# Retention and token/channel mixer on one core: two u turns by crossbar, a last chain in halves, another order

## The chip, the cores and the metric

The kernel runs on one core of a Trainium2 chip. The metric is the device time of one execution in microseconds; of several executions the median is given. A separate execution is profiled: its page and its trace are what the sections below read. Engines are TensorE (PE, with its weight loads as PEld), VectorE (DVE), ScalarE (ACT), GpSimd (POOL) and SyncE (SP); POOL, SP and ACT also issue DMAs.

## What is computed

For each of 4 batches and 8 heads (sequence 768, head size 64) a decaying state is carried along the sequence, and its output goes through a mixer over tokens and one over channels:

```python
gamma = 1.0 - 2.0 ** (-5.0 - np.arange(H, dtype=np.float32))
for t in range(S):
    state = gamma * state + k[:, :, t] (outer) v[:, :, t]
    y[:, :, t] = scale * q[:, :, t] @ state
...
xt = x.transpose(0, 2, 1)                  # x: heads side by side, 512 wide
h = np.maximum(xt @ w_tok1, 0.0) @ w_tok2  # 768 -> 256 -> 768
u = x + h.transpose(0, 2, 1)
h2 = np.maximum(u @ w_ch1, 0.0) @ w_ch2    # 512 -> 1536 -> 512
return u + h2
```

(The two lines in the loop are abridged.) Inputs and output are float32, products run on float16.

## The kernel before

The sequence is cut into six chunks of 128, the heads into four pairs of 128 rows. For each batch b and pair p, `front(b, p)` does the retention and the token mixer; for each batch, `back(b)` does the channel mixer.

**front.** q, k and v come by POOL's DMAs, which convert to float16 (`load`); only k of pair (0,0) comes through SP as float32. `decayed` scales k, and q where it will be turned by crossbar, by powers of the head's gamma (L530 on ScalarE, L532 on VectorE). `turn` brings k and q into columns: by six or twelve TensorE transposes and a copy out of PSUM (modes "t" and "w"), or by a crossbar DMA on SP (mode "x", L544). The table `TURNS` gives a mode for k, q and u of each pair: batches 0 and 1 have `twt`, batches 2 and 3 `xxx`. Then: state contributions per chunk (L586, half the array's columns at a time), a first copy and four decaying sums on VectorE (L596, L598), crossing states (L616, L618), scores (L637, half the rows), the mask (L648), y from scores and from states (L668, L694), copies out (L710), the token mixer (L725, relu L734 or L736, L745), and u (L710), which is turned too: by six transposes (L790) with a copy (L796), or by crossbar (L780).

**back.** The first channel product ("widen") is done plainly for batch 0 (L824, relu L840); batches 1 to 3 save one product in eight by sums and differences of blocks (`widen7`): differences of u on VectorE (L863), products (L893), kept parts copied by ScalarE (L904), added (L913) and clipped in place (L917) by VectorE. The first product of a batch waits for u of all its four pairs. The second product ("narrow") is done in the same way for block pairs (`narrow7`: sums L1007, chains of six matmuls of 256 columns L1043 and L1053, kept parts L1033, additions into X L1060, and a store of 128 rows, 256 KB, L1086). For the last batch, blocks 4 and 5 go plainly through `narrow` (L969, L978, store L984), the last of them in column pieces of 256, 128 and 128.

**Order.** Every piece of work is an `Op` with one or more ways (an engine, a cost in ns, the code that issues it). Two long strings give the order of all of them (`ORDERED`, an index of two digits each) and the way of each (`WAYS`). `arrange` walks through the order with a model of engines, PSUM banks, buffers and DMA rings to place banks and buffers, and each engine gets its instructions in that order, in its own queue; an engine waits at each instruction until what it needs is there. Until 21 us of planned time, fill matmuls on a zero tile (L1168) are put where the plan has gaps on TensorE.

**Constants.** `away` (POOL iota, L402) is a table of column minus row; from it come the logarithms `lgs` of the decays (eight memsets L408, a product L410 on VectorE), and from these the factors `gk` for k (L414) and `gy` for q (L415) on ScalarE, the identity (L418) and the mask (L444). `late`, q's decay along the chunk, is four exponentials on ScalarE (L435).

Of the kernel before, what the change touches and what calls it, by code (L numbers as in the profile page):

```python
# [9 lines left out]
FP = mybir.dt.float32  # L10
# [28 lines left out]
class Rings:  # L39
# [67 lines left out]
INTO, OUT_OF = 92, 111  # L107
FREE = dict(PE=300, ACT=2500, DVE=900, POOL=900, SP=750)


def arrange(ops, BANKS, seq, ways):
# [82 lines left out]
    while left:  # L194
        moved = False
        wake = INF
        for e in ENGINES:
# [61 lines left out]
    "0b05040a07000d0103020e060c1e0h1f1i0f1j1g1h0j08090g1t1k1x1s1l0i1O1m1w1P1n1v0l1Q1o1u1S1R1p1y1T0o1z1q1U1r1V221W"  # L259
    "230n2o1A1X242p1Y0m1C1Z2q26202s272r1B2t0k1D2Y252C2D2Z0q2F2u212H302v2G28312a2w292E0r2b2c1E2x2y0t2I2z1F2d342A35"  # L260
    "0p2B1J362e37380s2K1G2f2M2J392L1H2g3a0w2N321I1K2j332h2O0v2i1L3c2P4K0A2k3e3d3b2Q3f2m3h0u2R2T2l3g3i3k1M2U3m3j3l"
    "0z2V1N5j3n3C4L3y3o2S0y3z2W2n3p3A47483q2X0x3t5k3r493u3E3B0E3s3w3vac3xaf3F3GaM3HaN3DadaPaO0Dagaear4aaxah3IaQ0C"
    "3Jas3Mat4baR3Pb73Qb8b13Nau0B3Oavb24cawaD3KaJ0Gayb3aGb9aKazao0F3L4laLaH4oap4n0L4daq3R3TaI4eaA1a3VaBaS4H4GaT4f"
    "ai4maUaj0H4gaE4pak4I4hal4i4J1bbjamaFaVbkan1d3SaC0JbaaWbm3Ubbbo3Wb4aXaYbnb5bc1caZ4jbg0Nb0bd16bh3Xbi0K17b6be3Y"
    "bqbl18bf0I3Z4UbI40bObr19410R424k4Y4M5fbvbP4V4r4t4Nbw4q6p4sbx4X0M4u4Obz4v4Pby43154Wbs5Obp45bA4Q44bBbJ5gbt4w46"
    "4RbKbE4xbL4SbTbCbF4T4Z50bU4y5P0T5152bD4z5Q5l5U4A5m4B0O535V5h5W4CbX5n5X540Pc44DbM5o5ibY555Y5pbNc56mc85q5Z56bR"
    "bu6qc65r575R5Sc95t5sbS5T5a585vcd6n5ubV6r5wce605y5x5AchbQ5C6oc7bW5z5Bci5b0Q6s6Uc06t5D594E5c0U6ucmc17s6v6V5E6w"
    "12cn4F6xcfbZ5F0S617t62cg5G6y640W5J5H665dcj655K145I635e5Mck68670X5N69ca6bcl5L6a0Vcb6A6ccqcu6X6C6d6Y6DcNcc6Z6e"
    "cLcrcvcwcM6B6f6z6WczcscQcxcA6icRct707u6gcCcOcTcD6EcBcUcScycocEcJ806GcV6I6jd0716hcKcGd1cXcH81d26FcY6kdR116H72"
    "d3d4cW736Jd9cZ74d7dS13d5dT6KdWd8d6dU7y7vda757zdX6L7AdbcFcPdZ767Bdcdhe0dY7w6Mde7C0Z7xdie1e683djcI7De3dfe76N6l"  # L270
    "e4dk78dV77dAdd7cdoc2dB6Q7bcp6OdC7982dpdFe5dq6RdDdldG7adrdIdEdsdm7e7gdJdHdt6S86dn84dydK7d7f87dzdP850Y886PdMdL"
    "89ey7hdu8adQe26TdNdv7ieWdg8yeu7j7EdwbGez8bc3eUeX7kev8B7Gew8C7l7K7FeDeQ8zeFdOdxeE7I8A7oeV7meGeHex7peJeS8c7reR"
    "7qeAeI7J7nf1eB8D96eK7M7O7HeMeLbHeZeNf27L7Nf0eC8e107Pe8f37Q8i99f58ff48h7R9a8g8dee9be97Secf697ef9E7TeY8jea8k7U"
    "7Wf7ed8m7V8Eeg9c7XeTej9H7Z9d8F7Y8l9eeh8G9f8Hf898ekeieb8nen8I8of9el9g8J9h8peoemfc8Mep8q8Keq8O8L8r8Qfg8P8s8uer"
    "fx8t8Nfh9kfdfyfi8v9nflfjfCfmfz9mfD8Sfofe8wfO9lfpfF9F8R9ofvfGfA8U9G8Tfn9ifffE8VfqfMfwg58xfH8Wfs9IfN9Kft9jfJ9J"
    "8X9Lfkg6fKfQ9MfP8Ygaetfug7fRgbfT9N9qgdfU9O9p9PeO9r8Zg8gegc9Q90fW9t9s92fX9ufVgfgk91g3fY93ghfIg4g0fBgi949vglg1"
    "gD9w9SgEg2fSgmgg9R9UgIgn9xg9fZgFgJ9Tgr9y9VgLgsgtfrgGgMgKgu9z9W9XgN9ZgvgSgogwgTgBa19AgxgOgCgPfLgp9YgyhChIhEa0"
    "hGgza2gjhNhDhHgQa3gqgHhLhOa4hg9BhRhM9DhFa5hPhJa6hifbgYhSgRhrgAhQhha8hUhTa9hkhsabgUhvgVgZa7h095hK9Ch3hlh1hjfa"
    "hmh4gWePhphnh2h5hqhogXh7h6hth8hVh9huhwhchxhyhahYi2hZiAhbi3ijaai4hdi7ikhei0ilesi8i5iohAi9hzipiahWimhfiqhXi1ir"
    "ibiHisicihiTitiiieivifiRiwiCiBj8iSiFiYiDiGiWiUhBiyi6iIiXidjaixiziJiZjfiKj0kEiPiMj1iQj6iNj3jpj2j9j4koj7jdjbjq"  # L280
    "jrinjejwjujsjgjvkMkNkpjhjciEjxiVjtjniLjyjKiujojEigjik6jFjzjkjjkqjAjlkFkOkwk2kPkQkGjBk3k7kriOjCkRksjmkbk4jDkt"
    "j5kcjGkdjHjLkHkIkfkejIjPkSkujMjJkvjRjNkTk5khjQkgjSjTkijVkjjUkJkxkmjWjYjOkKk8jXkLkyjZkzk0k9kAk1kBkkkakCklkDkn"
)
WAYS = (
    "000000000000000000000000000000000000000000000000000000000000000000000000000010000000000000000000000000000010"
    "010100000000000000000000000001010000000100000000000000000000000000000000000100000000000010000000000010000000"
    "000101010000000000000000000000000000000010100000000000000000000000000000001000000000000000000000000000010100"
    "000000000000001000000000000000000001010110000000000000000000000000000000010000000000000000000000000000000000"
    "000000000000000000000000000000010010000000000000000000000000000000000000000000000000000000000000000000000000"
    "000000000000000010000000000000000000000000000000001000000000001000000010000000000000000000000000000000000000"  # L290
    "000000000000000000000000000000000000000000000000000000000000000000000000000011000000000000000000001100000000"
    "000000000000110000000000000000000010000000000000000000000000000000000000000000000000000000000000000000000000"
    "000000000000000000000000000000001100000000000000000000000000000000000000000010000000000000000000000000000000"
    "000000000000000001000000000000000000000000000000000000000000000000000000000000000000000000100000100000000000"
    "000000000010000000000010001000001100000000000000000000000000000000000001000000000000000000100000000000000000"
    "000010000000001000000100000000000000000000000000000010000000000000000000000100000000000000000000000100000000"
# [4 lines left out]
def kernel(  # L301
# [43 lines left out]
    TURNS = "twt twt twt twt twt twt twt twt xxx xxx xxx xxx xxx xxx xxx xxx".split()  # L345
# [39 lines left out]
    lgs = const_p.tile([P, H], FP, name="lgs")  # L385
    lnsc = const_p.tile([P, 1], FP, name="lnsc")
# [31 lines left out]
    ident_op = prep("DVE", 330, lambda: nc.vector.tensor_scalar(ident16, away, 0.0, None, ALU.is_equal), [away_op],  # L418
                    (-20, 0, -1, 1))
# [781 lines left out]
```

## Time and profile before

| | |
|---|---|
| median of 3 runs | 187.42 us (186.85 to 187.65) |
| profiled execution | 186.83 us |
| its span, first to last instruction | 185.0 us |
| granted TensorE clock | 0.996 |
| instructions | 5291 |
| moved by DMA | 24.91 MB in 92248 packets |

The page gives busy time by engine, the span in 40 slices, the DMA queues, and the chain of work that ended last, followed back from the last instruction. A matmul's duration holds its way through the array, so that neighbours overlap; what one costs in a row of matmuls is the distance from start to start. The chain of waits gives each piece from its release on. Every time in a timeline counts from the span's start.

### The profile page before, as it was taken

The numbers are of one execution on the slowest core, as the hardware profiler recorded it, in microseconds if no ns is written. First come the engines' busy times: TensorE is split into PE (matmuls) and PEld (weight loads), VectorE is DVE, ScalarE is ACT, GpSimd is POOL, SyncE is SP. The second block draws the span as 40 slices with busy tenths as digits, with TensorE's granted clock in tenths as the row PEclk, the third lists the DMA queues.
The fourth block names the chain that finished last, engine by engine and source line by source line (L and its number), as shares of the span: only waits on it lengthen the run. The fifth ranks groups of instructions, "written<-read, shape, count | busy, mean of one in ns | idle before, by whom it ended". The sixth has DMA issues, their size and how long they took to land.

```text
span 185.0 us, 5291 instructions
## 1 busy us (share of the span) xinstructions
PE 177.1 (96%) x2089; PEld 134.6 (73%) x2089; DVE 170.2 (92%) x466; ACT 133.4 (72%) x304; POOL 53.6 (29%) x63
## 2 busy tenths in 40 slices
PE   7788899999999999999999999999999999999991
PEld 3456788656689988866668898667679986567881
DVE  4599799859999999999999999999999999999992
ACT  5689698469789899999999697898864416552120
POOL 8994786355424609704220020000000000000000
PEclk9999999999999999999999999999999999999998
DMA  6999999999999999999999995027002444500035
GB/s 117 143 160 176 199 170 198 194 189 206 167 157 154 121 156 123 156 148 185 146 233 161 190 138 100 4 43 198 3 0 40 123 143 174 225 0 0 4 142 198
DMA packets 92248, 24.91 MB, mean 135 GB/s; under 512 B 81984, under 2 KB 89280, under 8 KB 92224
## 3 DMA queue, kind: packets, MB, share of 16 engines
q0 software_dynamic: 67728, 13.18, 89.8%
q1 hardware_dynamic: 23056, 9.11, 25.4%
q10 hardware_dynamic: 1440, 2.29, 3.3%
q8 instruction: 16, 0.26, 0.6%
q14 instruction: 8, 0.07, 0.1%
HBM read 26.74 MB, written 6.29 MB: 179 GB/s over the span
## 4 chain that ended last, share of the span: by engine, by line
PE 69%; DVE 16%; POOL 6%; DMA 5%; issue 2%; ACT 1%; POOLq 0%
PE bank L893 18%; PE bank L1043 11%; PE bank L824 9%; PE bank L1053 9%; DMA wt<-in_moe_w_tok_dram 5%; PE bank L745 5%; PE bank L725 4%; DVE X L1060 4%; DVE am L648 4%; DVE hs L1007 3%; PE bank L969 3%; DVE h L913 2%; POOL v L492 2%; PE bank L668 2%; PE bank L637 2%; PE bank L694 2%
## 5 line engine op out<-in xcount | busy, mean ns | idle before, releaser
L648 DVE TENSOR_TENSOR am<-bank,mask 128x384 f16<-128x384 f32 x64 | 32.9, 547 | 2.9 <-PE bank L637 2.8
L913 DVE TENSOR_TENSOR h<-bank,us 128x384 f16<-128x384 f32 x54 | 28.8, 551 | 0.6 <-PE bank L893 0.2
L904 ACT COPY us<-bank 128x384 f32<-128x384 f32 x50 | 23.3, 489 | 8.3 <-PE bank L893 6.4
L492 POOL DMA_DIRECT2D v<-in_v_dram x16 | 16.5, 1034 | 40.4 <-PE bank L694 25.7
L893 PE MATMUL bank<-hs,late 128*128 128x384 f16 x108 | 22.6, 326 | 0.0
L1033 ACT COPY us<-bank 128x256 f32<-128x256 f32 x30 | 10.7, 373 | 14.5 <-PE bank L1043 9.5
L1043 PEld LDWEIGHTS <-hs 128*128 128x128 f16 x198 | 18.5, 98 | 2.4
L893 PEld LDWEIGHTS <-late 128*128 128x128 f16 x144 | 13.2, 98 | 8.2 <-issue 0.4
L1060 DVE TENSOR_TENSOR X<-X,bank 128x256 f32<-128x256 f32 x44 | 17.7, 412 | 0.8 <-PE bank L1053 0.4
L1043 PE MATMUL bank<-wsum,hs 128*128 128x256 f16 x132 | 17.5, 273 | 0.0
L598 DVE SCALAR_TENSOR_TENSOR U<-U,gp,bank 128x64 f32<-128x64 f32 x64 | 16.8, 274 | 0.7
L710 ACT CAST u<-bank 128x384 f16<-128x384 f32 x31 | 14.6, 487 | 3.9 <-PE bank L745 3.3
L824 PE MATMUL bank<-uT,wc 128*128 128x384 f16 x96 | 16.9, 326 | 0.0
L492 POOL DMA_DIRECT2D k<-in_k_dram x15 | 15.4, 1033 | 4.9 <-DVE am L648 1.4
L710 ACT CAST x<-bank 128x384 f16<-128x384 f32 x30 | 14.1, 483 | 3.6 <-PE bank L694 3.4
L893 PE MATMUL bank<-uT,wc 128*128 128x384 f16 x72 | 16.4, 326 | 0.1
L616 ACT ACTIVATE cross<-U,gp 64x320 f16<-64x320 f32 x29 | 16.2, 559 | 0.4
L745 PE MATMUL bank<-h,wt 128*128 128x128 f16 x192 | 15.7, 219 | 0.3 <-DMA wt<-in_moe_w_tok_dram 0.3
L530 ACT ACTIVATE k<-k,gk 128x384 f16<-128x384 f16 x25 | 14.9, 617 | 1.4 <-DMA k<-in_k_dram 1.1
L840 ACT ACTIVATE h<-bank 128x384 f16<-128x384 f32 x24 | 10.6, 492 | 5.0 <-PE bank L824 4.8
L710 ACT COPY X<-bank 128x384 f32<-128x384 f32 x29 | 14.0, 492 | 0.0
L745 PEld LDWEIGHTS <-wt 128*128 128x128 f16 x192 | 12.3, 98 | 2.2 <-DMA wt<-in_moe_w_tok_dram 0.5
(91 smaller groups left out, 382.8 us busy)
## 6 DMA issues: line engine op xcount, KB each, us to landing
out_dram<-X SPq DMA_DIRECT2D x15, 256.0 KB, 3.1
q<-in_q_dram POOLq DMA_DIRECT2D x16, 192.0 KB, 8.4
v<-in_v_dram POOLq DMA_DIRECT2D x16, 192.0 KB, 7.3
k<-in_k_dram POOLq DMA_DIRECT2D x15, 192.0 KB, 7.9
wc<-in_moe_w_ch_dram POOLq DMA_DIRECT2D x5, 512.0 KB, 13.9
out_dram<-X ACTq DMA_DIRECT2D x8, 256.0 KB, 2.5
wc<-in_moe_w_ch_dram POOLq DMA_DIRECT2D x2, 256.0 KB, 10.6
us<-in_k_dram SPq DMA_DIRECT2D x1, 384.0 KB, 3.4
```

Source lines behind the costliest of these rows:

```text
L492: (nc.sync if hard else nc.gpsimd).dma_start(out=tile_of(s, [P, 2, NC, D], FP if hard else F16), in_=src.rearrange("h (c p) d -> p (h c) d ...
L598: nc.vector.scalar_tensor_tensor(out=u[:, c], in0=u[:, c - 1], scalar=gp[:, p:p + 1], in1=st, op0=ALU.mult, op1=ALU.add)
L648: nc.vector.tensor_tensor(am, SC[g].tile[:, :m * P].rearrange("p (i t) -> p i t", t=P), mask.to_broadcast([P, m, P]), ALU.mult)
L710: (nc.scalar.copy if e == "ACT" else nc.vector.tensor_copy)(tile(), t)
L745: nc.tensor.matmul(Y[j].tile[:, 2 * i * D:2 * (i + 1) * D], wt2[:, jt, t], H1.tile[:, jt], start=False, stop=(jt == NJ - 1), skip_group_ch ...
L824: nc.tensor.matmul(acc[:, :SH], wc1[:, ct, ft * P:(ft + 1) * P], UT.tile[:, ct, sh * SH:(sh + 1) * SH], start=(ct == 0), stop=(ct == NP - 1))
L893: nc.tensor.matmul(acc[:, :SH], left(ct), r[:, ct], start=first and ct == 0, stop=ct == C2 - 1, skip_group_check=True)
L904: (nc.scalar.copy if e == "ACT" else nc.vector.tensor_copy)(ks[:, j], R1.tile[:, :SH])
L913: nc.vector.tensor_tensor(h(m, sh), R.tile[:, :SH], KS.tile[:, j], ALU.add)
L1043: nc.tensor.matmul(acc_[:, lo], l[:, j], r[:, j], start=first and j == 0, stop=j == K2 - 1, skip_group_check=True)
L1053: nc.tensor.matmul(acc_[:, lo], l[:, j], r[:, j], start=first and j == 0, stop=j == K2 - 1, skip_group_check=True)
L1060: (nc.vector if e == "DVE" else nc.gpsimd).tensor_tensor(dst(), dst(), b_(), ALU.add)
```

## The change

- **u by crossbar.** `TURNS` has `twx` for pairs 0 and 1 of batch 1: their u is turned by a crossbar DMA on SP.
- **The last chain in two halves.** In `narrow7` for blocks 2 and 3 of the last batch, the last chain (columns 256 to 511 of block 2) is split into two of 128 columns, each with its own addition and its own store of 64 KB. The first 256 columns of block 2 are stored by themselves (128 KB), block 3 as a whole (256 KB).
- **k decays from ScalarE.** `gk` is computed by one activation from the logarithms (`lnG`) with `away` as its scale; `lgs`, the product on VectorE, is left for `gy` only, and `late` waits for the memsets only.
- **More choice.** The first state copy (L596) and the in-place relu of `widen7` (L917) may also go to ScalarE.
- **Costs and order.** Costs of the planner are changed (among them the price of a change of tile shape on TensorE, and the landing of POOL's loads until 26 us); `ORDERED` and `WAYS` are new throughout. By position, TensorE has 446 groups instead of 447. POOL issues k and q of pair (0,1) and v of pair (0,0) ahead of `away`, q of pair (0,3) ahead of the first token weight, and v of pair (0,3) behind the second. Five stores of batches 1 and 2 stand among the last work of batch 3.

```diff
-            return 1470 if t < 4500 else 2100 if t < 17000 else 1700
+            return 1470 if t < 4500 else 2100 if t < 26000 else 1700
...
-INTO, OUT_OF = 92, 111
-FREE = dict(PE=300, ACT=2500, DVE=900, POOL=900, SP=750)
+CHANGE = {"": 92, "row": 110, "col": 100, "turn": 110}
+FREE = dict(PE=300, ACT=2100, DVE=900, POOL=900, SP=750)
...
-                    s_ = max(t, free[e] + (INTO if o.tiled else 0) + (OUT_OF if tiled == "high" else 0))
+                    s_ = max(t, free[e] + CHANGE[tiled])
...
-    TURNS = "twt twt twt twt twt twt twt twt xxx xxx xxx xxx xxx xxx xxx xxx".split()
+    TURNS = "twt twt twt twt twx twx twt twt xxx xxx xxx xxx xxx xxx xxx xxx".split()
...
-            nc.vector.memset(lgs[:, h:h + 1], math.log(1.0 - 2.0 ** (-5.0 - h)))
+            nc.vector.memset(lnG[:, h:h + 1], math.log(1.0 - 2.0 ** (-5.0 - h)))
         nc.vector.memset(lnsc, math.log(scale))
-        nc.vector.tensor_scalar(lgs, lgs, away[:, MID:MID + 1], -1.0, ALU.mult, ALU.mult)
-    lgs_op = prep("DVE", 450, emit, [away_op])
-
-    def emit():
-        nc.scalar.activation(gk, lgs, AF.Exp, scale=-1.0)
-        nc.scalar.activation(gy, lgs, AF.Exp, bias=lnsc, scale=1.0)
-    g_op = prep("ACT", 380, emit, [lgs_op])
+    logs_op = prep("DVE", 220, emit)
+    lgs_op = prep("DVE", 400, lambda: nc.vector.tensor_scalar(lgs, lnG, away[:, MID:MID + 1], -1.0, ALU.mult, ALU.mult),
+                  [away_op, logs_op])
+    g_op = prep("ACT", 190, lambda: nc.scalar.activation(gk, lnG, AF.Exp, scale=away[:, MID:MID + 1]), [away_op, logs_op])
+    gy_op = prep("ACT", 190, lambda: nc.scalar.activation(gy, lgs, AF.Exp, bias=lnsc, scale=1.0), [lgs_op])
...
-    gq_op = prep("ACT", 2450, emit, [since_op, lnh_op, lgs_op], (-20, 0, -1, 1), [LATE], [SINCE])
+    gq_op = prep("ACT", 2450, emit, [since_op, lnh_op, logs_op], (-20, 0, -1, 1), [LATE], [SINCE])
...
-                    nc.vector.tensor_copy(u[:, 0], st)
+                    (nc.scalar.copy if e == "ACT" else nc.vector.tensor_copy)(u[:, 0], st)
...
-                    def emit():
-                        nc.vector.tensor_scalar(h(m, sh), h(m, sh), 0.0, None, ALU.max)
-                    rel[i + m * M2, sh] = op(one("DVE", (180, 260), emit), [ad], [], [H2s[sh]])
+                    def emit(e):
+                        if e == "ACT":
+                            nc.scalar.activation(h(m, sh), h(m, sh), AF.Relu)
+                        else:
+                            nc.vector.tensor_scalar(h(m, sh), h(m, sh), 0.0, None, ALU.max)
+                    rel[i + m * M2, sh] = op(either(emit, DVE=(167, 250), ACT=act(SH, 0, 1)), [ad], [], [H2s[sh]])
...
-            p3 = chain(lambda: HS.tile[:, 3], w(1, hi), [sm[3], k4] + cw, False, True)
-            o12 = add(part(x0, hi), acc(0, lo), [p3] + xd, [X, banks[0]], FROM_BANK)
...
+            if b == B - 1 and i1 == 3:
+                store(i1, slice(0, C), [y2])
+                store(i0, lo, [y11])
+                got = k4
+                for g in range(2):
+                    cols = slice(g * P, (g + 1) * P)
+
+                    def emit(cols=cols, left=lambda: HS.tile[:, 3], right=w(1, hi)):
+                        l, r = left(), right()
+                        for j in range(K2):
+                            nc.tensor.matmul(banks[0].tile[:, cols], l[:, j], r[:, j, cols], start=False, stop=j == K2 - 1,
+                                             skip_group_check=True)
+                    got = op(one("PE", (336, 500), emit), [sm[3], got] + cw, [], [ha, hb, HS, banks[0]])
+                    last = slice(N2 + g * P, N2 + (g + 1) * P)
+                    o12 = add(part(x0, last), lambda cols=cols: banks[0].tile[:, cols], [got] + xd, [X, banks[0]],
+                              dict(DVE=(200, 284)))
+                    store(i0, last, [o12])
+            else:
+                p3 = chain(lambda: HS.tile[:, 3], w(1, hi), [sm[3], k4] + cw, False, True)
+                o12 = add(part(x0, hi), acc(0, lo), [p3] + xd, [X, banks[0]], FROM_BANK)
+                store(i1, slice(0, C), [y2])
+                store(i0, slice(0, C), [y11, o12])
```

The rest of the diff is the two strings and planner costs that change by a few ns.

More of the change, by code (lines that the diff above doesn't have):

```diff
@@ L264 @@
[L264 to L273, printed above, removed]
@@ L599, in emit @@
                                                    op0=ALU.mult, op1=ALU.add)
-            prev = op(one("DVE", (195, 280) if c else (140, 220), emit), [pp, gp_op, prev], [US] if c == 0 else [],
+            prev = op(either(emit, DVE=(190, 276)) if c else either(emit, DVE=(132, 216), ACT=act(D)), [pp, gp_op, prev], [US] if c == 0 else [],
                       ([] if c == 0 else [US]) + [ST])
@@ L796, in emit @@
                 (nc.scalar.copy if e == "ACT" else nc.vector.tensor_copy)(UT.tile[:, p], T.tile[:, :S])
-            e = op(either(emit, ACT=act(S), DVE=dve(S, 0.54)), [t, None if opens else first_of[b, "uT"]],
+            e = op(either(emit, ACT=act(S), DVE=(467, 550)), [t, None if opens else first_of[b, "uT"]],
                    [UT] if opens else [], [T] if opens else [T, UT])
@@ L1044, in emit @@
                                          stop=j == K2 - 1, skip_group_check=True)
-                return op(one("PE", (655, 815), emit), deps, [banks[0]] if first else [],
+                return op(one("PE", (655, 818), emit), deps, [banks[0]] if first else [],
                           [ha, hb, HS] if first else [ha, hb, HS, banks[0]])
@@ L1054, in emit @@
                                          stop=j == K2 - 1, skip_group_check=True)
-                return op(one("PE", (655, 815), emit), deps, [banks[g]] if first else [],
+                return op(one("PE", (655, 818), emit), deps, [banks[g]] if first else [],
                           [ha, hb, HS] if first else [ha, hb, HS, banks[g]])
```

105 lines of the change are left out of this document (59 added, 46 removed).

## The prediction

> **What bounds the kernel now.** I read the page first, then the chain of waits, the busy time by stretches, the waits on TensorE, and the timeline where the change touches it.
>
> ```profile
> span 185.0 us, 5291 instructions
> ...
> PE 177.1 (96%) x2089; PEld 134.6 (73%) x2089; DVE 170.2 (92%) x466; ACT 133.4 (72%) x304; POOL 53.6 (29%) x63
> ...
> PE 69%; DVE 16%; POOL 6%; DMA 5%; issue 2%; ACT 1%; POOLq 0%
> ```
>
> The span is 185.0 us; the profiled execution itself took 186.83, so 1.8 us lie around the span, and the median of the runs shown, 187.42, stands 0.6 above that execution. I sum against the span and carry both offsets to the end. TensorE holds 69% of the chain that ended last, VectorE 16%.
>
> ```profile
> 11.65 9.10 DMA wt<-in_moe_w_tok_dram
> 20.80 0.51 PE bank L745 x6
> ...
> 49.99 0.67 PE bank L725 x12
> ...
> 180.63 0.67 PE bank L1043 x6
> 181.32 0.42 DVE X L1060
> ```
>
> The chain in order of time has three parts: a start that waits for the token weights until 20.80, a long body, and a tail behind the last chain of matmuls, which hands over at T = 181.30.
>
> ```profile
> 85.00:119.00 34.00, 33.98 (x428) 27.11 (x426) 33.82 (x100) 30.12 (x74) 4.91 (x5) 1.00 1.15 151
> 119.00:155.00 36.00, 35.96 (x364) 27.60 (x365) 34.75 (x92) 23.08 (x56) 0.00 (x0) 1.00 0.28 71
> 155.00:181.00 26.00, 26.00 (x203) 18.76 (x203) 25.08 (x67) 9.80 (x23) 0.00 (x0) 1.00 0.27 102
> ```
>
> Columns: length, then PE, PEld, DVE, ACT, POOL busy, granted clock, DMA. TensorE is busy all through, at full clock; VectorE nearly so; ScalarE has room only after 119. From 25 to 181.5 the waits of the weight loads are small, and most are TensorE's own:
>
> ```profile
> PEld L637 <- issue: 1.7, 6, 0.3
> ...
> PEld L893 <- DVE hs L863: 0.4, 1, 0.4
> ```
>
> So the body is priced in TensorE time, and work taken from VectorE or ScalarE counts only where TensorE was waiting for it.
>
> **The change, part by part.**
>
> *u of pairs (1,0) and (1,1) by crossbar.* Removed are two groups of six transposes and their two copies on ScalarE; added are two crossbar DMAs on SP.
>
> ```profile
> 56.98 0.50 PE L790 MATMUL bank<-ident,u 128*128 128x128 f16 x6
> 57.31 0.82 PE L1053 MATMUL bank<-wsum,h 128*128 128x256 f16 x6
> ...
> 70.26 0.50 PE L790 MATMUL bank<-ident,u 128*128 128x128 f16 x6
> 70.60 0.82 PE L1043 MATMUL bank<-wc,hs 128*128 128x256 f16 x6
> ...
> 76.94 0.50 PE L893 MATMUL bank<-uT,wc 128*128 128x384 f16 x2
> ```
>
> From start to the next start a group holds TensorE 0.33 and 0.34 us: together -0.67. The batch's first reader on TensorE comes at 76.94. Is the crossbar in time?
>
> ```profile
> 69.31 0.55 DVE L710 CAST u<-bank 128x384 f16<-128x384 f32 x1
> ...
> 76.78 0.55 DVE L863 TENSOR_TENSOR hs<-uT 128x768 f16<-128x768 f16 x1
> ```
>
> ```profile
> kT<-k SPq DMA_TRANSPOSE x8, 5.0
> ...
> uT<-u SPq DMA_TRANSPOSE x8, 2.9
> ```
>
> u of pair (1,1) is whole at 69.9; a crossbar takes a median of 2.9 (u, later, on quiet queues) to 5.0 us (k, among the loads) to land: 72.8 to 74.9, 1.9 us or more before the difference on VectorE wants it. Pair (1,0) has 13 us more. In SP's new order they stand behind the second and the fifth of batch 2's crossbars; whatever blocks one blocks all behind it. I take 0 for lateness, with 2 us as the upper end (a further pair of crossbars of 192 KB served first). The loads behind which they squeeze have slack, since POOL waits for free buffers, not for the ring:
>
> ```profile
> POOL v L492 <- PE bank L694: 25.7, 4, 9.5
> ```
>
>
> *Fewer changes of tile shape.* The new string orders TensorE's groups so that it passes between full, row (L637), column (L586) and half-width (L554) tiles 64 times instead of 71; behind the first widen matmul it is 39 instead of 43.
>
> ```profile
> 51.97 0.44 PE bank L637 x12
> 52.41 0.76 PE bank L1053 x6
> ...
> 72.09 0.65 PE bank L1053 x6
> 72.74 0.44 PE bank L637 x12
> ```
>
> The same six matmuls take 0.76 behind L637 and 0.65 behind full tiles: 0.11 a change. Four in the body: -0.44, from 0 to -0.77 (all seven).
>
> *VectorE against ScalarE.* Counted off the strings, 21 of the in-place relus (L917) and 12 of the first state copies (L596) go to ScalarE, 17 decays (L530/L532) come from it to VectorE and 6 go back; other moves nearly cancel. With
>
> ```profile
> L917 DVE TENSOR_SCALAR h<-h 128x384 f16<-128x384 f16 x54 | 12.3, 259 | 0.1
> ...
> L596 DVE COPY U<-bank 128x64 f32<-128x64 f32 x16 | 3.4, 215 | 0.4 <-PE bank L586 0.3
> ...
> L532 DVE TENSOR_SCALAR q<-q,gy 128x384 f16<-128x384 f16 x5 | 1.5, 309 | 0.0
> ```
>
> VectorE loses 21 x 0.26 + 12 x 0.215 - 11 x 0.31 = 4.6 us of 170. A relu on ScalarE isn't in the trace; it lies between the 0.26 of VectorE and the 0.49 that its relus from PSUM take, and ScalarE's room behind 119 hides it. But in 85 to 119, where the chain rides VectorE, six relus and some four copies leave (-2.4) and about as many decays arrive (+2.5 for eight net): I take 0, from -1.0 to +1.0 if the few releases there come earlier or later.
>
> *The start.* k's factors no longer wait for the product on VectorE, but POOL now issues three more loads (of up to 1.02 us each) ahead of the index table.
>
> ```profile
> 2.20 0.26 POOL L402 IOTA away<- 128x128 f32 x1
> 2.39 1.02 POOL L492 DMA_DIRECT2D v<-in_v_dram  x1
> ...
> 2.97 0.51 DVE L418 TENSOR_SCALAR ident<-away 128x128 f16<-128x128 f32 x1
> ...
> 5.99 0.59 PE L554 MATMUL bank<-ident,q 128*64 128x128 f16 x12 [0.52 <-DMA q<-in_q_dram]
> ```
>
> Up to 3.1 us later, the table is there by 5.5 and the identity by 6.1, level with the q load that the first transposes wait for (5.99); a few tenths are covered by the wait for the weights at 20.80. For those, one q load moves ahead of the first weight and one v load behind the second: one against one, 192 KB each. I take 0, from -0.6 to +0.6, half of one load's time at the some 1.2 us that the ring needs for 192 KB at 160 GB/s.
>
> *The tail.* The last chain's six matmuls of 256 columns become twice six of 128: twelve of 128 take 0.67 (L725 above), as the chain does: 0. What follows it:
>
> ```profile
> 178.83 0.28 DVE L978 TENSOR_TENSOR X<-X,bank 128x128 f32<-128x128 f32 x1
> ...
> 181.77 0.33 SPq L1086 DMA_DIRECT2D out_dram<-X  x1
> ```
>
> ```profile
> out_dram<-X SPq DMA_DIRECT2D x1, 256.0 KB, 2.0
> ```
>
> ```profile
> out_dram<-X SPq DMA_DIRECT2D x1, 64.0 KB, 1.6
> ```
>
> Now: 0.42 for the add, 0.03, 2.0 to landing (issued 181.77, landed 183.8), then 1.2 to the span's end: T + 3.7. With 128 columns: 0.28 + 0.03 + 1.6 + 1.2 = T + 3.1. But the new order also holds stores back: five of batches 1 and 2, of 256 KB each, go out in the last 7.4 us. From the first of that train to the end stand eight chains (8 x 0.65), the two halves (0.67) and 1.3 us of narrow pieces on TensorE, and 12 x 256 KB of stores, where the present end has 6.
>
> ```profile
> GB/s 0 0 0 0 0 0 0 55 300 423 382 396 328 382 410 396 355 383 410 382 355 369 423 382 341 396 383 396 355 396 410 383 341 396 410 151 0 0 0 0
> ...
> out_dram<-X SPq DMA_DIRECT2D x5, 256.0 KB, 2.5
> ```
>
> This is the DMA view of 154 to 160, 0.15 us a slice: six stores flow 28 slices, 4.2 us, 0.70 each, starting 0.85 after the first issue at 154.35. So the train flows from T - 7.4 + 0.85 = T - 6.5 for 12 x 0.70 = 8.4 us to T + 1.9; with some 0.35 to land (a lone store: 2.0 less 0.75 and the flow of 0.9) and 1.2 it ends at T + 3.45: -0.25 instead of -0.6. I take -0.25; the ends are -0.6 and the rival below.
>
> The Trainium skill speaks against this tail: DMA: Bandwidth & Descriptors, Specifications, puts the limit of a core's HBM at about 358 GB/s. By it 3.15 MB take 8.8 us instead of 8.4 and the tail gains nothing; the slices above, 380 on their mean, lie over it.
>
> **Sum:** -0.67 - 0.44 + 0 + 0 - 0.25 = -1.36: span 183.6, that execution 185.5, median 186.1.
>
> **Rivals.**
> - *More.* Start and VectorE both fall at their good ends (-0.6, -1.0): 184.5 to 185.3, say 184.9. For it: VectorE is lighter by 4.6 us. Against it: TensorE hardly waits as it is.
> - *The gain goes into new waits.* Nearly every group moves, and a just-in-time order has hardly any cover; at the bad ends of start and VectorE (+0.6, +1.0) the sum is +0.24: 187.7. For it: VectorE stays full from 85 to 119.
> - *The store train is the bound (slower).* A lone 256 KB store flows 0.9 us, and small rows and two queues may do no better. At 0.92 the train ends at -6.5 + 11.0 = T + 4.5, +0.35 + 1.2 = T + 6.1, 2.4 later than now: -1.1 + 2.4, 188.7. It costs more than everything else brings once a store takes over 0.81: then 12 x 0.81 = 9.7, and T + 4.8 eats the 1.1. Against it: 0.70 in the one train shown.
> - *The crossbar is late.* TensorE stands some 2 us at the first widen product of batch 1: -1.36 + 2 = +0.6, 188.1. For it: k crossbars amid the loads take 5.0.
>
> **Chances.** Forecast 0.48, more 0.12, new waits 0.17, store train 0.15, crossbar 0.08. A measurement of this kernel can tell about 0.5%, 0.94 us, from no change. The forecast's own range is 185.3 to 186.9 (its unknown costs mostly offset each other), so of its 0.48 some 0.38 is faster and 0.10 same; all of "more" is faster; new waits give 0.02, 0.10, 0.05; the last two are slower. Faster 0.52, same 0.20, slower 0.28. Range: 184.8 leaves out about half of "more", 188.2 about two thirds of the store train: with the tails, under 0.2.
>
> **What would show it.** Six fewer transposes twice at L790, and no TensorE wait for the crossbar near 77: first term. The first widen matmul (31.7 now) and the last TensorE group each say what start and body did: I expect T near 180.2. The last landing minus T: 2.25 or less if the train keeps 0.70. Wrong if T doesn't fall by over 0.5, or if the span ends more than 4 us behind T, or if TensorE shows waits of over 1 us in the body.

## The result, and the profile after

The kernel after takes 186.05 us in the median of 14 executions (185.63 to 187.1); the kernel before, on the same chip, 187.19 (186.83 to 187.94). The ratio is 0.9942, with a 95% interval of 0.9924 to 0.996: 1.1 us faster. The forecast was 186.1.

The profiled execution of the kernel after took 186.50 us, 0.45 above its median. These rows of its page answer to the first ones of before:

```profile
span 184.7 us, 5303 instructions
...
PE 176.6 (96%) x2088; PEld 134.2 (73%) x2088; DVE 168.9 (91%) x446; ACT 137.6 (74%) x323; POOL 53.9 (29%) x63
...
PE 67%; issue 11%; POOL 11%; DMA 9%; ACTq 0%; ACT 0%; DVE 0%; POOLq 0%
```

In the chain of work that ended last, VectorE has gone from 16% to nothing, DMA from 5% to 9%, and the loads' issue by POOL and idle time that nothing explains ("issue") from 6% and 2% to 11% each. ScalarE carries 4.2 us more. The busy time by stretches (length, then PE, PEld, DVE, ACT, POOL, granted clock, DMA) shows where to look for the new DMA share:

```profile
85.00:119.00 34.00, 33.06 (x407) 26.74 (x407) 33.24 (x94) 29.33 (x75) 6.22 (x6) 1.00 1.40 174
119.00:155.00 36.00, 36.00 (x376) 27.90 (x376) 34.22 (x85) 25.49 (x65) 0.00 (x0) 1.00 0.21 50
155.00:181.00 26.00, 26.00 (x208) 18.75 (x206) 23.94 (x62) 12.45 (x29) 0.00 (x0) 1.00 0.31 115
```

From 85 to 119 TensorE is busy for 33.06 of 34 us; before it was 33.98. The chain of waits and the timeline show the missing piece:

```profile
96.45 7.14 DMA k<-in_k_dram
```

```profile
103.23 0.51 PE L638 MATMUL bank<-qT,kT 64*128 64x128 f16 x12
...
103.62 0.61 ACT L531 ACTIVATE k<-k,gk 128x384 f16<-128x384 f16 x1 [1.50 <-DMA k<-in_k_dram]
...
104.14 0.35 ACT L1037 COPY us<-bank 128x256 f32<-128x256 f32 x1
...
104.54 0.81 PE L1047 MATMUL bank<-wc,hs 128*128 128x256 f16 x6 [0.80 <-ACT us L1037]
```

ScalarE stands 1.50 us at the decay of k (L531) for a load that lands 7.1 us after its issue (5.9 to 6.2 in five other profiles of this order). Behind it in ScalarE's queue is the copy of a kept part (L1037), and TensorE waits 0.80 for that copy. (Lines of after lie a few higher than those of before: L1047 is L1043, L1057 is L1053, L638 is L637, L746 is L745.)

**Where the time went.** For each profile I took the matmuls behind the first widen matmul, counted each at the distance from start to start that its shape keeps in an undisturbed row (0.163 us for 384 columns, 0.109 for 256, and so on), and each change of tile shape at 0.105; what is left over is TensorE waiting.

| us, or a number (changes of shape) | before | after | after, second profile |
|---|---|---|---|
| first widen matmul starts | 31.66 | 31.55 | 31.18 |
| from there to the last matmul | 149.36 | 149.66 | 149.66 |
| of it matmuls | 143.75 | 143.24 | 143.24 |
| changes of shape in it (number) | 43 | 39 | 39 |
| of it waiting | 1.14 | 2.38 | 2.38 |
| last matmul to the span's end | 4.02 | 3.51 | 3.57 |
| span | 185.0 | 184.7 | 184.4 |

The body has 0.51 less matmul time (0.67 by the two crossbars; 0.16 came back, most of it because ten more of the small matmuls at L587 stand behind the first widen matmul) and four changes of shape less (0.42), and 1.24 more waiting: it is not shorter. In eight profiles with the new order, runs below included, the same 1650 matmuls follow each other, so they can be lined up one by one. Against the median of the eight, after stands 0.87 us at 104.5, and the second profile 0.44 at 56.1 and 0.44 at 60.1: the waits for loads are 0.87 and 0.88 of the 1.24. Where the other 0.36 lies was not found. What the span gained came from the end (0.45 to 0.51) and from the start (0.11 to 0.48). Between the two profiled executions of before and after this makes 0.3; the rest of the 1.14 is that the one lay 0.36 below its median and the other 0.45 above.

The end of after, in the timeline and in the view of the DMAs (the last number is the median from issue to landing):

```profile
180.36 1.75 SPq L1086 DMA_DIRECT2D out_dram<-X  x3
...
180.90 0.34 ACTq L1086 DMA_DIRECT2D out_dram<-X  x1
...
181.45 0.34 ACTq L988 DMA_DIRECT2D out_dram<-X  x1
181.46 0.29 DVE L1064 TENSOR_TENSOR X<-X,bank 128x128 f32<-128x128 f32 x1
```

```profile
out_dram<-X SPq DMA_DIRECT2D x1, 64.0 KB, 2.0
```

The last chain hands over at T = 181.44; the last store is issued at 181.78 and lands at 183.75, T + 2.3 (before: T + 2.5). The 64 KB take 2.0 us to land, as long as 256 KB took before.

### The profile page after: what moved, and what is told of

It is laid out like the page before. It is cut to its first block, busy times and chain, and to the rows that moved or that the text cites. A ratio compares the mean times of both kernels' runs of the same rounds, so it can differ in the third digit from the quotient of the medians.

```text
span 184.7 us, 5303 instructions
## 1 busy us (share of the span) xinstructions
PE 176.6 (96%) x2088; PEld 134.2 (73%) x2088; DVE 168.9 (91%) x446; ACT 137.6 (74%) x323; POOL 53.9 (29%) x63
## 4 chain that ended last, share of the span: by engine, by line
PE 67%; issue 11%; POOL 11%; DMA 9%; ACTq 0%; ACT 0%; DVE 0%; POOLq 0%
PE bank L894 15%; PE bank L1047 14%; PE bank L1057 9%; PE bank L825 9%; DMA v<-in_v_dram 5%; PE bank L746 4%; DMA k<-in_k_dram 4%; PE bank L726 4%; POOL k L493 3%; PE bank L973 3%; POOL v L493 3%; PE bank L669 2%; PE bank L638 2%; POOL q L490 2%; POOL q L493 2%
## 5 line engine op out<-in xcount | busy, mean ns | idle before, releaser
L1037 ACT COPY us<-bank 128x256 f32<-128x256 f32 x27 | 10.1, 377 | 14.6 <-PE bank L1047 13.3
L1047 PEld LDWEIGHTS <-hs 128*128 128x128 f16 x192 | 18.1, 98 | 2.9 <-issue 0.8
L1064 DVE TENSOR_TENSOR X<-X,bank 128x256 f32<-128x256 f32 (+1 forms) x45 | 17.8, 407 | 1.4 <-PE bank L1057 1.0
L1047 PE MATMUL bank<-wsum,hs 128*128 128x256 f16 x132 | 17.6, 273 | 0.0
L825 PE MATMUL bank<-uT,wc 128*128 128x384 f16 x96 | 17.6, 326 | 0.0
L617 ACT ACTIVATE cross<-U,gp 64x320 f16<-64x320 f32 x28 | 15.7, 559 | 2.5 <-DVE U L599 2.0
L894 PE MATMUL bank<-uT,wc 128*128 128x384 f16 x72 | 16.5, 326 | 0.0
L711 ACT CAST u<-bank 128x384 f16<-128x384 f32 x28 | 13.4, 482 | 3.3 <-PE bank L746 3.2
L746 PE MATMUL bank<-h,wt 128*128 128x128 f16 x192 | 15.2, 219 | 0.1
L711 ACT COPY X<-bank 128x384 f32<-128x384 f32 x31 | 14.7, 489 | 0.4 <-DVE u L711 0.4
L894 PEld LDWEIGHTS <-wc 128*128 128x128 f16 x108 | 9.9, 98 | 5.7
L726 PE MATMUL bank<-x,wt 128*128 128x128 f16 x192 | 13.4, 219 | 0.6 <-DMA wt<-in_moe_w_tok_dram 0.5
L711 ACT CAST x<-bank 128x384 f16<-128x384 f32 x28 | 13.0, 492 | 1.2 <-PE bank L695 1.2
L746 PEld LDWEIGHTS <-wt 128*128 128x128 f16 x192 | 12.3, 98 | 2.1 <-DMA wt<-in_moe_w_tok_dram 0.2
```

Of the source, the lines that this page charges most:

```text
L711: (nc.scalar.copy if e == "ACT" else nc.vector.tensor_copy)(tile(), t)
L726: nc.tensor.matmul(acc[:, jt * P:(jt + 1) * P], wt1[:, i, jt * P:(jt + 1) * P], X16.tile[:, i].rearrange("p h d -> p (h d)"), start=(i == ...
L746: nc.tensor.matmul(Y[j].tile[:, 2 * i * D:2 * (i + 1) * D], wt2[:, jt, t], H1.tile[:, jt], start=False, stop=(jt == NJ - 1), skip_group_ch ...
L825: nc.tensor.matmul(acc[:, :SH], wc1[:, ct, ft * P:(ft + 1) * P], UT.tile[:, ct, sh * SH:(sh + 1) * SH], start=(ct == 0), stop=(ct == NP - 1))
L894: nc.tensor.matmul(acc[:, :SH], left(ct), r[:, ct], start=first and ct == 0, stop=ct == C2 - 1, skip_group_check=True)
L1047: nc.tensor.matmul(acc_[:, lo], l[:, j], r[:, j], start=first and j == 0, stop=j == K2 - 1, skip_group_check=True)
```

## The experiments

A sequence number below is that of an operation in the kernel's list; `move(a, before)` takes operation `a` out of the order and puts it just ahead of the other. The edits are abridged. Times are medians; all ratios are to the kernel before, run on the same chip at the same time. The median of before was 187.07 to 187.19 each time, so times of different runs can be set side by side, within what medians of a few executions differ by.

**The kernel after once more** (no edit).

> The changed kernel as it is, profiled once more. The first profile has one wait that stands out: TensorE stands 0.88 us at 103 us, behind ScalarE, which itself waits 1.5 us for a load of k (landed at 103.6). Theory: the wait belongs to that execution, and the median lies below the profiled time because most executions don't have it; then TensorE hands over its last product about 0.8 us earlier (near 180.6) and no wait there is over 0.3 us. Rival: it belongs to the order (a load that this order always needs too early); then the wait comes back with 0.5 to 1.2 us at the same instruction.

Measured: 186.17 us (185.22 to 187.1, 12 executions), ratio 0.9948 [0.9929, 0.9966]. The wait at 103 is gone, and two others are there. In the timeline:

```profile
54.71 1.12 ACT L531 ACTIVATE k<-k,gk 128x384 f16<-128x384 f16 x2 [0.63 <-DMA k<-in_k_dram]
...
55.74 0.35 ACT L1037 COPY us<-bank 128x256 f32<-128x256 f32 x1
...
56.14 0.81 PE L1047 MATMUL bank<-wsum,hs 128*128 128x256 f16 x6 [0.28 <-ACT us L1037]
...
60.12 0.35 PE L587 MATMUL bank<-v,k 128*64 128x64 f16 x10 [0.27 <-DMA v<-in_v_dram]
```

The pattern is that of 103: a k decay on ScalarE waits for a load, a kept part waits behind it, TensorE waits for the kept part; and at 60.12 TensorE waits for a v load itself. Neither expectation was met: T is 181.06, not 180.6, and the wait is elsewhere. So the waits move between executions, with the landing of the loads, while their sum stays at 2.38.

**u of (1,0) and (1,1) back on TensorE.**

```diff
-    TURNS = "twt twt twt twt twx twx twt twt xxx xxx xxx xxx xxx xxx xxx xxx".split()
+    TURNS = "twt twt twt twt twt twt twt twt xxx xxx xxx xxx xxx xxx xxx xxx".split()
+    seq = [i + (i > 255) + (i > 289) for i in seq]     # each turn is two operations again
+    move(255, 284); move(290, 360)                     # the transposes
+    seq.insert(seq.index(713), 256); seq.insert(seq.index(410), 291)   # their copies
```

> The changed kernel, with u of pairs (1,0) and (1,1) turned on TensorE again. Theory: each group of six transposes costs TensorE 0.34 us and hides nothing, so it is 0.67 us slower than the changed kernel (0.3 to 1.2, since the order was not made for it). Rival: the transposes filled gaps of TensorE, or the crossbar brings as much waiting as it saves: no difference within 0.2 us.

Measured: 187.36 us (186.65 to 189.21), ratio 1.0018 [0.9991, 1.0045], 1.2 us above after. Each group of transposes holds TensorE for 0.33 us until the next start:

```profile
57.37 0.50 PE L791 MATMUL bank<-ident,u 128*128 128x128 f16 x6
...
57.70 0.83 PE L746 MATMUL bank<-h,wt 128*128 128x128 f16 x12
```

The matmul time of the body so rises by the predicted 0.67, from 143.24 to 143.91. The body itself is 149.86, only 0.21 longer than in after, because the waits for loads are 0.87 there and 0.44 here. With the matmuls lined up, what follows each group comes 0.33 us later and stays so, and the second run with u on TensorE (below), without such waits, has a body of 149.46, 0.71 above the 148.75 of the three moves below, which has none either. So the 0.67 is real, but the profiles of this run and of after don't show it in their totals. The rest of the 1.2 has nothing to do with these transposes: from the last landing to the end of the span pass 1.66 us, against 0.97 in after. The run below on SP's instructions shows what that is.

**u of (1,0) and (1,1) by crossbar in the kernel before**, matmuls in the old order, only loads, crossbars and one sum of weights on VectorE moved (the expectation calls it a decay).

```diff
+    TURNS = "twt twt twt twt twx twx twt twt xxx xxx xxx xxx xxx xxx xxx xxx".split()
+    seq = [i - (i > 254) - (i > 289) for i in seq if i not in (254, 289)]
+    for a, before in [(62, 1261), (66, 1259), ...]:    # 40 moves: 23 loads, 16 crossbars, 1 sum of weights
+        move(a, before)
```

> The kernel before with u of pairs (1,0) and (1,1) turned by crossbar, its matmuls and VectorE work in the old order; only DMA issues (POOL's loads and SP's crossbars) and one decay are moved so that the two crossbars find room. Theory (the twelve transposes are worth their 0.67 us of TensorE wherever the crossbar is in time): 187.15 - 0.67 = 186.5 (186.2 to 186.8), TensorE's wait at the first widen product of batch 1 (near 76 us) under 0.2 us. Rival (the saving needs the new order: in the old one the crossbars or the loads that they push back are late): 187.0 to 187.8, with waits of 0.4 us or more between 70 and 85 us; the planner's own sum for this order is 183.81 against 183.76 before, which is with this rival. Besides, two DMAs more move the last store from the sixth last to the fourth last of the semaphores that SP goes through at the end, 0.06 us each: -0.12 in both.

Measured: 188.68 us (187.46 to 189.13), ratio 1.0057 [1.0031, 1.0082]: 1.5 us slower than before, worse than either expectation. From its waits and timeline:

```profile
PE bank L790 <- ACT u L710: 1.0, 1, 1.0
```

```profile
73.72 0.50 PE L790 MATMUL bank<-ident,u 128*128 128x128 f16 x6
...
75.30 0.86 ACT L710 CAST u<-bank 128x384 f16<-128x384 f32 x2 [1.69 <-DMA uT<-u]
75.83 0.72 PE L790 MATMUL bank<-ident,u 128*128 128x128 f16 x6 [0.95 <-ACT u L710]
```

The crossbar of u isn't late for its reader; it lands late for the next u. ScalarE can't write u of a later pair until the crossbar has read the buffer, and the crossbar of (1,0), issued at 69.05 behind those of batch 2, lands at 75.22. Six transposes hold a u buffer for 0.5 us, a crossbar for its whole way through the queue, here 6 us. The body is 1.4 us longer though it has 0.67 less matmul time, so 2.0 us of waiting are new; 0.95 of them stand at this place, the rest was not placed (and the first widen matmul came 0.6 later in this execution). In after the two crossbars are issued at 62.6 and 69.5, and no such wait shows.

**The six stores of batches 1 and 2 put ahead of the last part** (near 155 us instead of 174).

```diff
+    for i in (897, 918, 940, 941, 1068, 1090):
+        move(i, 1069)
```

> The changed kernel, with six stores of batches 1 and 2 (256 KB each) issued near 155 us instead of in the last 8 us. Theory: the train of stores is what ends the kernel; without it the last landing comes 2.05 us after the last product instead of 2.33, and the kernel is 0.3 us faster (0.2 to 0.5). Rival: the train drains before the last small store, and nothing changes (within 0.1 us).

Measured: 186.35 us (186.03 to 187.85), ratio 0.9953 [0.9931, 0.9976]: no difference to after. From 154 to 164 us the DMAs now move 212 GB/s (55 in after), from 172 to 184 only 133 (264), and yet the last landing stays at T + 2.32. So the train of stores was not what set the last landing.

**The k decay of 103 us behind the copy of the kept part.**

```diff
+    move(564, 485)
```

> The changed kernel, with one decay of k (batch 3, pair 2, first head) moved on ScalarE behind the kept copy and the first X copy that stood behind it. If the wait of 0.88 us at 103 us belongs to the order, TensorE doesn't wait there and the kernel is up to 0.9 us faster than the changed one; if it belongs to one execution, no difference in the median (within 0.2 us).

Measured: 186.4 us (185.65 to 186.58), ratio 0.9951 [0.9932, 0.997]. No wait at 103, but 0.21 and 0.44 at 56 and 60 us, where the second profile of after has its waits: again no difference.

**The tail alone, in the kernel before.** In `narrow7` of before the branch of the last batch was put in as in the change, then the end of the order was set:

```diff
+    seq = [...] + [1262, 1265, 1250, 1261, 1282, 1263, 1264, 1283, 1266, 1267]
     # chain a, chain b, add, store lo, add (block 5), add a, store a, store (block 5), add b, store b
```

> The kernel before with only the last chain in two halves and the small stores; no store held back. Theory: last landing minus the end of the last matmul 1.9 us (2.5 before), and 0.12 less behind it (two semaphores fewer to go through): 186.4 to 186.7. Rival (the landing of a small store is no shorter, or the two small stores queue behind the other stores of the end): last landing minus the end of the last matmul 2.3 to 2.5, time 186.9 to 187.2.

Measured: 187.75 us (187.32 to 188.66), ratio 1.0035 [1.0013, 1.0057]: slower than before. Two faults of my order show in the timeline: the store of block 5 (L984) stands behind the first small one on ScalarE, and goes out 0.7 us behind T (182.71 against 181.99) instead of 0.1 ahead of it. And SP's end took 1.68 us instead of 1.22. So it was run again with the block's store first, and with three stores of the middle on SP instead of ScalarE:

```diff
-    [..., 1282, 1263, 1264, 1283, 1266, 1267]
+    [..., 1282, 1283, 1263, 1264, 1266, 1267]
+    ways[918] = ways[919] = ways[941] = 1
```

> The kernel before with the last chain in two halves; the other last store (block 5) is issued ahead of the small ones on ScalarE, and three stores of the middle go through SP instead of ScalarE, so that SP's pause falls under the waits for the last stores. Theory (in b_tail_halves a queue order and SP's pause hid the gain): last landing minus the end of the last matmul 1.9 to 2.2 us, end of the span 1.1 us behind it, time 186.4 to 186.8. Rival (halves save nothing at the end): 2.5 us, time 187.0 to 187.3.

Measured: 187.63 us (186.99 to 188.24), ratio 1.0032 [1.0004, 1.006]. The last landing is at T + 2.41, and 1.56 us more to the end: by the landing the rival is right, halves put in by themselves save 0.1 us of it; the time lies above both expectations. The timeline:

```profile
180.74 0.83 PE L1096 MATMUL bank<-wc,hs 128*128 128x128 f16 x12
...
181.03 0.41 DVE L978 TENSOR_TENSOR X<-X,bank 128x256 f32<-128x256 f32 x1
...
181.61 0.48 DVE L1060 TENSOR_TENSOR X<-X,bank 128x128 f32<-128x128 f32 x2 [0.17 <-PE bank L1096]
```

Issued back to back, both chains are done before the first addition starts: VectorE stands idle for 0.17, then does both additions in 0.48, more than the one of 256 columns took (0.42). That the two chains write one bank may be why the first addition waits for both; no run tried two banks. In the kernel after the halves start 1.5 us apart, with another chain (L1047) and narrow pieces (L973) between them, so that the first addition and store run under these.

**The start: index table and k's factors early.**

```diff
+    move(0, 16)    # away second on POOL, as before
+    move(3, 8)     # gk ahead of late on ScalarE
```

> The kernel after with the index table second on POOL (as before) and k's factors ahead of late on ScalarE. Theory (the start is covered by the wait for the token weights): 186.1 (185.8 to 186.4), first L746 within 0.3 us of 20.95. Rival (the later factors and table cost the start up to 0.6): 185.5 to 185.7, and the first widen matmul 0.4 us or more earlier than 31.55.

Measured: 186.36 us (185.82 to 187.14), ratio 0.9955 [0.9937, 0.9973]: as after. By the median the theory holds: the start is covered. Its mark, the first L746 within 0.3 us of 20.95, was missed in the one profile, an execution 0.64 above its median: it came at 22.0, as in others (see the last section).

**Relus and first copies back on VectorE, order kept.**

```diff
+    for o in ops:
+        if [w[0] for w in o.ways] == ["DVE", "ACT"]:   # L921/L919 and L597
+            ways[o.n] = 0
```

> The kernel after with all 21 in-place relus and 12 first state copies back on VectorE (order unchanged): some 8 us more on VectorE, less on ScalarE. Theory as predicted (moving them was worth about 0, at most 1.0): 186.1 to 187.1. Rival (VectorE is the bound where they stand, and the order stands only with them on ScalarE): 187.5 to 188.6, with TensorE waiting for VectorE between 85 and 150 us; the planner's own sum is 2.4 us longer.

Measured: 189.13 us (188.81 to 190.03), ratio 1.0105 [1.0076, 1.0135]: 3.0 us above after. The profiled execution is the slowest (190.03): its first widen matmul comes at 33.25, 1.7 us later than in after, and its body is 151.45, 1.8 longer, of it 4.17 waiting. Page and timeline:

```profile
PE 180.1 (96%) x2090; PEld 135.4 (72%) x2090; DVE 174.0 (92%) x479; ACT 129.2 (69%) x290; POOL 53.9 (29%) x63
```

```profile
101.54 0.32 PE L638 MATMUL bank<-qT,kT 64*128 64x128 f16 x5 [0.36 <-DVE X L1064]
...
103.42 0.81 PE L1057 MATMUL bank<-wsum,hs 128*128 128x256 f16 x6 [0.41 <-DVE am L649]
```

VectorE is busy 5.1 us longer, and the kernel takes 3.0 more, in part by a later start and in part by waits for VectorE in the body. It is a bound just below the surface: the work can't go back to it in this order.

**Three moves where the loads were late.**

```diff
+    for a, before in (51, 50), (714, 360), (564, 485):
+        move(a, before)    # k load behind two v loads; two kept copies ahead of k decays
```

> The kernel after with three moves at the places where TensorE waited for loads: k of pair (2,1) is loaded behind two v loads, so that these land one load's turn (1.3 us) earlier, and the kept-part copies near 55 and 102 us go ahead of the k decays on ScalarE. Theory (the waits of 0.4 to 0.9 us at 55, 59 and 103 us come from loads that land late and from k decays that wait for them in front of a copy): no wait of over 0.3 us between 50 and 110 us, body from the first widen matmul to the last matmul 148.6 to 149.0 us (149.66 in two profiles of the kernel after), time 185.3 to 185.8. Rival (another load is late in their place): body 149.4 or more, time 186.0 to 186.3.

Measured: 186.0 us (185.34 to 186.32, 6 executions), ratio 0.9938 [0.9913, 0.9964]. In the profiled execution, its fastest (185.34), the waits are gone: body 148.75, waiting 1.47. At the place that waited 0.80 before:

```profile
101.61 0.37 ACT L1037 COPY us<-bank 128x256 f32<-128x256 f32 x1
102.10 0.61 ACT L531 ACTIVATE k<-k,gk 128x384 f16<-128x384 f16 x1
...
103.23 0.83 PE L1047 MATMUL bank<-wc,hs 128*128 128x256 f16 x6
```

The copy goes first, and TensorE does not wait. T is 180.14, near the 180.2 that the prediction expected of the change. The mechanism is shown in the trace, but the median lies in the rival's range and can't be told from that of after: four of its six executions lie between 185.8 and 186.32. What those waited for, no profile shows.

**SP's instructions: two stores less on SP.** Nothing else differs from after.

```diff
+    ways[1069] = ways[1091] = 0
```

> The kernel after with two stores of the middle issued by ScalarE instead of SP; nothing else differs. Theory (SP pauses some 0.45 us behind its 79th instruction; with four instructions less that is behind the last landing): from last landing to the end of the span 1.3 to 1.5 us instead of 0.98, time 186.4 to 186.7. Rival (no such pause): 0.98 us, time 186.1.

Measured: 186.95 us (186.73 to 187.23), ratio 0.9995 [0.9973, 1.0016]; 1.56 us from the last landing to the end instead of 0.97. SP's records there in the trace (its number, what it waits for, from and to):

```
79 wait S[118]   184.01 to 184.04
80 drain S[99]   184.48 to 184.62
81 drain S[97]   184.69 to 184.69
```

and those of after:

```
79 wait S[114]   182.51 to 182.54
80 wait S[115]   183.36 to 183.39
81 wait S[116]   183.57 to 183.59
82 wait S[117]   183.77 to 183.79
83 wait S[118]   183.83 to 183.86
84 drain S[99]   183.90 to 183.91
85 drain S[97]   183.96 to 183.97
```

Between instructions 79 and 80 SP pauses for 0.44 us, and the drain behind it takes 0.14 instead of 0.01. In after number 80 waits for a store anyway, and the pause lies under that wait. The median rose by 0.8 to 0.9, more than the 0.6 of the end; the remainder is within what medians of these runs differ by.

**u on TensorE again, four stores on SP.**

```diff
+    ways[748] = ways[749] = ways[770] = ways[1114] = 1    # in a_u_tensor
```

> The kernel after with u of (1,0) and (1,1) turned by TensorE, as in a_u_tensor, and four stores issued by SP instead of ScalarE, so that SP has as many or more instructions as in the kernel after. Theory (of the 1.2 us that a_u_tensor lay above the kernel after, 0.46 is a pause of SP behind its 79th instruction, which came behind the last landing there and comes under the wait for the last stores here): from last landing to the end of the span 1.1 to 1.2 us instead of 1.66, time 186.8 to 187.0. Rival (the pause is no matter of the instruction's place): 1.6 us again, time 187.3.

Measured: 187.52 us (186.4 to 188.06, 6 executions), ratio 1.0016 [0.9987, 1.0046]; 1.37 us from the last landing to the end. SP has 88 instructions, but the pause reaches past the last landing by some 0.25 us, so only part of it is covered; by the median the rival (187.3) is nearer than the theory. The profiled execution was the fastest of the six and says little of them.

## Why the prediction was right, and where it was not

The number was right, the distribution was not. The prediction's own test was that T falls by more than 0.5; it went from 181.30 to 181.44 and 181.06 in the two profiles, so by that mark the account failed. In the profiles the gain lies at the start and the end, which had been put at 0 and -0.25, and none of it in the body. That the sum came within 0.1 of the median is in part luck: waits that it didn't have ate the body's gain, gains that it didn't have took its place, and the median of before was 187.19, not the 187.42 of its first three runs, so that the change was -1.14 where -1.36 was forecast.

- **u by crossbar, -0.67.** Right, and shown by undoing it: each group that comes back puts all that follows 0.33 later. The crossbars, behind the first and the fourth of batch 2's and not the second and fifth, land at 66.9 and 75.2 (72.8 to 74.9 was forecast for the second); the first widen product of batch 1 starts without a wait:

```profile
77.39 0.86 PE L894 MATMUL bank<-uT,wc 128*128 128x384 f16 x4
...
77.63 0.55 DVE L864 TENSOR_TENSOR hs<-uT 128x768 f16<-128x768 f16 x1
```

  What the step did not see is the buffer: in the old order the kernel with the same two crossbars takes 1.5 us more, and the longest of its new waits comes from u staying occupied until one lands. The removal was worth its 0.67 in the order made for it; moving only loads, crossbars and a sum into the old one did not bring it.
- **Changes of tile shape, -0.44.** Right in number in the body: 43 became 39, 0.42 at the 0.105 of one. No run undid them by themselves. Over the whole kernel they went from 71 to 67, not to 64.
- **VectorE, 0 (-1.0 to +1.0).** Here a count failed. VectorE was to lose 4.6 us and lost 1.3:

```profile
L919 ACT ACTIVATE h<-h 128x384 f16<-128x384 f16 x21 | 10.8, 534 | 0.1
...
L533 DVE TENSOR_SCALAR k<-k,gk 128x384 f16<-128x384 f16 x14 | 5.4, 390 | 0.0
...
L711 DVE CAST u<-bank 128x384 f16<-128x384 f32 x4 | 2.2, 546 | 0.0
L711 DVE CAST x<-bank 128x384 f16<-128x384 f32 x4 | 2.2, 546 | 0.0
```

  A k decay on VectorE takes 0.39, not the 0.31 of q's (the page of before had five of k at 0.415), and "other moves nearly cancel" was wrong: eight casts of 0.55 stand on VectorE, three before, against one copy of X instead of three. A relu on ScalarE takes 0.534, above the upper bound of 0.49. In net time 0 may stand, but not as a term by itself: with the relus and copies back on VectorE the same order takes 3.0 us more, and the bound given was 1.0.
- **New waits, a rival with a chance of 0.17.** This is the step that failed: the sum had none in the body, and 1.24 us came, 0.87 of them from loads that land too late for the order, at two of the three places with a k decay in front of a kept-part copy. The prediction's mark for "wrong" was a wait of over 1 us; the longest was 0.87. The rival named start and VectorE as the place; it was the loads. In the one profile of the three moves, where they are gone, the body is 0.61 shorter than before, over half of the 1.11 that the sum had there.
- **The start, 0.** Right within its ends in the two profiles of after: the first widen matmul comes 0.1 to 0.5 earlier, and moving table and factors forward changes nothing in the median. In three other profiles of the new order it comes 0.6 to 1.0 later than before.
- **The tail, -0.25.** The size came from the wrong mechanism. The train did flow as forecast: from 175 to 180 us the DMAs move 381 GB/s, 0.69 us for 256 KB (0.70 forecast; it holds six stores of batches 1 and 2, not five, but the twelve stores of the sum are right), and the last landing came at T + 2.3 (2.25 forecast). But without the train it comes at T + 2.32. What stands ahead of it in both is the end itself: in after the 256 KB of another block are issued at 181.26 and land at 183.34, and the last two stores of 64 KB land behind them at 183.55 and 183.75. So the lone landing of 1.6 us does not apply to the last small store; that the block's store is what holds it is read from this order of landings, no run was made without it. By the page "DMA: Bandwidth & Descriptors", Specifications, of the Trainium skill (about 358 GB/s) the tail would have gained nothing. The 381 GB/s of this trace lie over that, as the slices of before did (their mean is 373, not 380), and the run without the train shows that the time did not hang on it.
- **Behind the last landing, taken as 1.2 in both.** It fell to 0.97, which no step had. In before, the last store signals semaphore 113, and SP then goes through 114 to 118 at 0.06 us each; in after it signals 117, and one is left. SP's records of before:

```
70 wait S[113]   183.83 to 183.85
71 wait S[114]   183.89 to 183.92
...
75 wait S[118]   184.13 to 184.16
```

  Four waits less are 0.24, and the end behind the landing is 0.25 shorter. The run of the crossbars in the old order has two more DMAs and signals 115: 1.09.

Open is how the medians' 1.14 us divide. The three profiles of kernels with the old body (before and the two tail runs) have their last matmul at 181.0, 181.7 and 181.4; the six of kernels with the new body (after twice, and the runs with the stores, the 103-us decay, the start and SP) at 181.2, 180.8, 181.0, 180.7, 181.7 and 181.3. The means differ by 0.2, and those of one kind spread by 0.7 to 1.0. The 0.5 from the last matmul to the span's end stands in five of these six (the run on SP's instructions loses it again); some 0.4 of the 1.14 stays without a place on which the profiles agree.

## What to carry to other kernels

A transpose that goes from TensorE to a DMA frees its third of a microsecond only if the source buffer can be held until the DMA has landed: count the buffers as well as the reader. In an engine's queue, an instruction that waits for a load belongs behind those that other engines wait for, even if the load is planned to be early. When a number comes out right, check its steps: here, in the profiles, two gains that were not foreseen covered one that didn't arrive.

## What the runs showed of the hardware

- **SP pauses at one place of its instruction stream.** Behind its 79th instruction it stands for 0.44 to 0.46 us without a recorded wait, in all five profiles where nothing covers the place (83, 84, 84, 86 and, in part, 88 instructions on SP). With 88, as in after, the pause lies under the wait for the last stores; with 79, in the run of the crossbars in the old order, it does not occur, and 1.09 us pass to the end. In before, with 80, the place coincides with the 0.45 to 0.46 us that lie ahead of SP's last record in every profile. What SP does in the pause no run shows.
- **The order of the semaphores counts at the end.** SP waits for them in a fixed order, 0.06 us each, so which of them the last store signals, and with it the number of DMAs before it, moves the end by up to 0.3 us (1.22 us behind the last landing with semaphore 113, 1.09 with 115, 0.97 with 117).
- **Starts fall into two groups.** The first L746 came at 20.9 in six profiles of the new kernels (the two of after, the 103-us decay, the three moves and both runs with u on TensorE), and at 22.0 in three (the stores, the start, SP); with the relus on VectorE it came at 22.6. In the three late ones the body was shorter (148.76 to 149.06, against 149.41 to 149.66 in the two of after and that of the 103-us decay, with the same matmuls after an early start), and the waits for loads at 56, 60 and 104 are not there. That the loads have caught up by then is our reading. In the old order no such difference shows (149.43 with a first widen matmul at 32.32, 149.36 and 149.74 with one at 31.66 and 31.61).
